# Queries, keys and values of two pairs per load, last tokens in token-major order, and expert weights issued from pair 22

## The chip, the cores and the metric

One Trainium2 chip, one NeuronCore. The time is device microseconds of one execution of the program; the kernel before takes 402.2 us, the median of three runs (401.68 to 403.0).

## The reference

Attention with a relative position bias, then a mixture of experts with hash routing. There are 8 batches, 8 heads, 576 tokens and a head dimension of 64, all inputs in float32.

```
scores = q @ k.T / 8 + bias_table[bucket(|i - j|)]     # per batch and head, 576 x 576
attn   = softmax(scores);  x = attn @ v                # x: 4608 tokens x 512
e      = token_ids * 2654435761 % 8                    # expert of each token
out    = relu(x @ w1[e]) @ w2[e]                       # w1: 512 x 1024, w2: 1024 x 512
```

## The kernel before

The work goes by pairs of heads: 8 batches of 4 pairs, 32 pairs. Of a head's 576 tokens 512 are held as 2 tiles (`NT`) of 128 partitions, each partition with two neighbouring tokens (512 bytes in float32). The last 64 tokens of each head, 32 double rows (`RU`), are packed for all four pairs of a batch into one tile, the "rest".

For each pair GpSimd casts q, k and v from float32 to float16 (`cast_qk`, L225; `cast_v`, L236), TensorE transposes q and k (`transpose_qk`, L370), and VectorE copies the results out of PSUM. Then come five steps g of scores: products of q and k, the bias added by further matmuls, and one exponential of 128x1024 on ScalarE (L506). The products with v (`av_steps`, L511) follow some one to two pairs later, nine matmuls at each step, and VectorE divides by the row sums (L546, L547) into `x_all`. The rest of a batch is cast by VectorE (`cast_rest`, L246, at step 3 of the second pair of the batch before it), transposed (`transpose_rest`, L388) and used with its batch.

The order of the work is written out by hand for all five engines (L580 to L769): what stands in the program is the order of each engine's queue. Loads, the rest, the token ids and the zero fills of the scatter table `t_xperm` stand in SyncE's queue. `pair_start(n)` (L693) puts there at the start of pair n: the rest of the next batch if n opens a batch (`load_rest`, L199, eight DMAs), q, k and v of pair n+4 (`load`, L183, six DMAs of 128 KB, one per tensor and head), the token ids at n = 4 (`route_load`, L264, six DMAs), and one fill of 514 KB for n from 2 to 11. A load waits until the buffer it overwrites (four per tensor, one pair each) has been cast. GpSimd gets at the same place the casts of q and k of pair n+3, from pair 12 on two indirect scatters of finished rows (`dispatch`, L561), and the first weights of two experts: w1 at pairs 20 and 25, w2 at pairs 22 and 28 (L713 to L720; 2 MB each in float32, cast to float16 on the way).

From pair 6 on the routing goes in small steps on VectorE, one per g. After the attention the experts run one after another on TensorE, with rows gathered by expert from `t_xperm`.

The prologue (L584 to L666) loads pairs 0 to 3, the rest of batch 0 and the bias tables in a written-out order on SyncE's and ScalarE's queues.

Of the kernel before, what the change touches and what calls it, by code (L numbers as in the profile page):

```python
# [11 lines left out]
F32 = mybir.dt.float32  # L12
# [19 lines left out]
def kernel(  # L32
# [11 lines left out]
    nc = tc.nc  # L44

    B, H, S, D = q.shape
# [6 lines left out]
    P = 128  # L53
    NPAIR = H // 2
# [95 lines left out]
    with tc.tile_pool(name="at", bufs=1) as at, tc.tile_pool(  # L150
# [29 lines left out]
        qf, kf, vf, qh, kh = {}, {}, {}, {}, {}  # L180
        qr, kr, vr = {}, {}, {}

        def load(n, which="qkv", eng=None):  # L183
            b, m = pairs[n]
            for key, dst, src in (("q", qf, q), ("k", kf, k), ("v", vf, v)):
                if key not in which:
                    continue
                dst[n] = at.tile([P, 2, NT, 2 * D], F32, name=key + "f",
                                 bufs=4)
                for hh in range(2):  # L190
                    (eng or nc.sync).dma_start(  # L191
                        out=dst[n][:, hh, :, :],
                        in_=bass.AP(
                            src.tensor, (b * H + 2 * m + hh) * S * D,
                            [[2 * D, P], [2 * P * D, NT], [1, 2 * D]],
                        ),
                    )

        def load_rest(b, which="qkv", eng=None):  # L199
            for key, dst, src in (("q", qr, q), ("k", kr, k)):  # L200
                if key not in which:
                    continue
                dst[b] = at.tile([P, 2, 2 * D], F32, name=key + "r", bufs=1)
                for hh in range(2):
                    (eng or nc.sync).dma_start(  # L205
                        out=dst[b][:, hh, :],
                        in_=bass.AP(
                            src.tensor, ((b * H + hh) * S + NB4) * D,
                            [[2 * S * D, NPAIR], [2 * D, RU], [1, 2 * D]],
                        ),  # L210
                    )
            if "v" in which:
                vr[b] = at.tile([P, NPAIR, D], F32, name="vr", bufs=1)
                for hh in range(2):
                    for c in range(2):
                        r0 = D * hh + RU * c
                        (eng or nc.sync).dma_start(  # L217
                            out=vr[b][r0 : r0 + RU, :, :],
                            in_=bass.AP(
                                v.tensor, ((b * H + hh) * S + NB4 + c) * D,  # L220
                                [[2 * D, RU], [2 * S * D, NPAIR], [1, D]],
                            ),
                        )

        def cast_qk(n, qeng=None, keng=None):  # L225
            for dst, src, name, eng in ((qh, qf, "qh", qeng),
                                        (kh, kf, "kh", keng)):
                dst[n] = at.tile([P, KT, 2, D], F16, name=name, bufs=2)
                (eng or nc.gpsimd).tensor_copy(  # L229
                    out=dst[n][:, :, :, :].transpose([0, 2, 1, 3]),  # L230
                    in_=src[n][:, :, :, :].rearrange(
                        "p h t (c d) -> p h (t c) d", c=2
                    ),
                )

        def cast_v(n):  # L236
            nc.gpsimd.tensor_copy(
                out=va[n % 3][:, :, :D],
                in_=vf[n][:, :, :, :].rearrange(
                    "p h t (c d) -> p (h t c) d", c=2  # L240
                ),
            )
# [145 lines left out]
        def transpose_rest(b):  # L388
            pr = aux(0, [P, 2, 2, P], F16, "pr")
            for i, key in enumerate("kq"):  # L390
                for c in range(2):
                    nc.tensor.transpose(
                        out=pr[:, i, c, :],
                        in_=rh[b, key][:, c, :, :].rearrange(
                            "p h d -> p (h d)"
                        ),
                        identity=ident[:, :],
                    )
            for hh in range(2):
                nc.vector.tensor_copy(  # L400
                    out=kzr[b % 2][D * hh : D * hh + D, :,
                                   D * hh : D * hh + D].rearrange(
                        "p m (c u) -> p c m u", c=2
                    ),
                    in_=pr[D * hh : D * hh + D, 0, :, :].rearrange(
                        "p c (m u) -> p c m u", m=NPAIR
                    ),
                )
            nc.vector.tensor_copy(
                out=qtr[b % 2][:, :, :].rearrange(  # L410
                    "p m (c u) -> p c m u", c=2
                ),
                in_=pr[:, 1, :, :].rearrange(
                    "p c (m u) -> p c m u", m=NPAIR
                ),
            )

# [163 lines left out]
            E_ALL.PE, E_ALL.Activation, E_ALL.Pool, E_ALL.SP, E_ALL.DVE,  # L581
        })
        guard.__enter__()
        load(0, "k")  # L584
        warm = at.tile([1, 1], F32, name="warm")
        nc.vector.memset(warm[:, :], 0.0)
        nc.scalar.activation(
# [6 lines left out]
        nc.gpsimd.memset(ebsb[:, :, :], 0.0)  # L594
        nc.scalar.dma_start(out=ohsb[:, :], in_=OH_d.ap())
        nc.scalar.dma_start(out=idents[:, :, :], in_=I128_d.ap())
        load(0, "q")
        load_rest(0, "kq", nc.scalar)

        cast_qk(0, nc.vector, nc.vector)  # L600
# [20 lines left out]
                ),  # L621
            )

        load(0, "v", nc.scalar)
        load_band(0, 2, nc.scalar)
        load(1, "qk")
        for hh in range(2):
            for c in range(2):
                r0 = D * hh + RU * c
# [25 lines left out]
        cast_v(0)  # L655
        load_band(2, 4, nc.sync)
        load_rest(0, "v")
        load(1, "v")
        cast_vrest(0)
        load(2)  # L660
        load_band(4, H, nc.sync)
        cast_qk(2)
        load(3)
        nc.sync.dma_start(out=msk[:, :], in_=MSK_d.ap())
        nc.sync.dma_start(out=cnt[:, :], in_=CNT_d.ap())
        nc.sync.dma_start(out=tok[:, :], in_=TOK_d.ap())  # L666

        FILLS = 10

# [23 lines left out]
        def pair_start(n):  # L693
            b, m = pairs[n]
            if b + 1 < B and m == 0:
                load_rest(b + 1)
            if n + 4 < NP:
                load(n + 4)
            if n == 4:
                route_load()  # L700
            if 2 <= n < 2 + FILLS:
                fill_table(n - 2)
            if n + 3 < NP:
                cast_qk(n + 3)
            if b + 1 < B and m == 2:
                cast_vrest(b + 1)
            if n >= 6 and pairs[n - 2][1] == 0:
                waiting.extend((pairs[n - 6][0], t) for t in range(NIT))
            if n >= 12:
                for _ in range(2 if n < NP - 2 else 4):  # L710
                    if waiting:
                        dispatch(*waiting.pop(0))
            if n == 20:  # L713
                load_w1(0)
            if n == 22:
                load_w2(0)
            if n == 25:
                load_w1(1)
            if n == 28:
                load_w2(1)  # L720

        def behind(n, g):
            G = NIT * n + g
# [261 lines left out]
```

## Time and profile before

| | before |
|---|---|
| median of three runs | 402.2 us |
| the profiled execution | 404.91 us, span 403.1 us |
| mean granted TensorE clock | 0.939 of full speed |
| busy: TensorE, ScalarE, GpSimd, VectorE | 338.6, 202.1, 160.9, 124.8 us |
| DMA | 72.87 MB in 94548 packets, 181 GB/s mean |

The span is what the hardware profiler saw of one execution; the execution's own time is slightly longer. PE is TensorE's matmul, PEld its weight loads, DVE VectorE, ACT ScalarE, POOL GpSimd and SP SyncE; a "q" behind the name is that engine's sequencer, which issues DMAs. L506 is line 506 of the kernel. Busy time is an average over attention and experts, which have different limits.

### The profile page before, as it was taken

Reading aid. Unit: us, or ns where it says so; the run is one execution under the profiler, and the core shown is the slowest. Engines: PE = TensorE matmul, PEld = TensorE weight load, DVE = VectorE, ACT = ScalarE, POOL = GpSimd, SP = SyncE. Lnnn points to the kernel's source line nnn. Section 1 sums busy time; section 2 is a strip of 40 time slices with the busy share of each in tenths; the row PEclk is TensorE's granted clock in tenths of the full one; section 3 lists DMA queues with packets and bytes.
Section 4 is the critical chain, followed back from the end, with each engine's and each line's share of the span. In section 5 each row is a group of like instructions: output and inputs, shape, how many; then the busy total and the mean of one; then the engine's idle time right before and its main releaser. Section 6 shows DMA issues by size and latency. Waiting matters only on the chain.

```text
span 403.1 us, 9232 instructions
## 1 busy us (share of the span) xinstructions
PE 338.6 (84%) x3796; PEld 210.3 (52%) x3796; DVE 124.8 (31%) x322; ACT 202.1 (50%) x235; POOL 160.9 (40%) x229
## 2 busy tenths in 40 slices
PE   2648994999999998688968708999999999999990
PEld 0224663566665664455545506665657565656650
DVE  2103442644343534134313301323141413223220
ACT  1262991898887879277847602231405051422310
POOL 6112413414358664591657230243343415141331
PEclk9995996899999999699989967999999999999997
DMA  5885958979694858987978143499999999996211
GB/s 155 204 226 167 251 157 197 266 192 269 179 271 140 240 176 181 261 144 185 196 209 136 51 126 116 76 205 154 262 170 248 216 184 270 152 261 117 89 69 63
DMA packets 94548, 72.87 MB, mean 181 GB/s; under 512 B 15223, under 2 KB 85655, under 8 KB 94496
## 3 DMA queue, kind: packets, MB, share of 16 engines
q1 hardware_dynamic: 74720, 40.13, 36.9%
q0 software_dynamic: 17664, 30.96, 36.8%
q10 hardware_dynamic: 2112, 1.09, 1.0%
q8 instruction: 32, 0.52, 0.6%
q14 instruction: 20, 0.16, 0.1%
HBM read 69.47 MB, written 21.03 MB: 225 GB/s over the span
## 4 chain that ended last, share of the span: by engine, by line
PE 61%; DMA 17%; SPq 10%; issue 4%; DVE 3%; POOL 2%; ACT 1%; ACTq 1%; POOLq 0%; DVEq 0%
PE hps L815 17%; PE ops L833 17%; PE px L537 7%; PE ps L441 7%; DMA kf<-in_k_dram 7%; PE ps L464 5%; SPq L191 5%; DMA kr<-in_k_dram 4%; PE pqk L376 3%; PE xps L794 2%; SPq L205 2%; SPq L217 2%; DMA xpn<-t_xperm 1%; DMA btb<-t_f 1%; DVE x_all L547 1%
## 5 line engine op out<-in xcount | busy, mean ns | idle before, releaser
L506 ACT ACTIVATE att<-ps 128x1024 f16<-128x1024 f32 x160 | 152.9, 1027 | 64.0 <-PE ps L464 41.8
L821 ACT ACTIVATE h<-hps 128x640 f16<-128x640 f32 x64 | 45.1, 704 | 112.8 <-PE hps L815 112.2
L441 PE MATMUL ps<-btb,idents 128*128 128x384 f16 (+1 forms) x384 | 80.0, 294 | 2.6 <-DMA btb<-t_f 2.3
L833 PE MATMUL ops<-w2t,h 128*128 128x512 f16 x320 | 72.7, 379 | 0.0
L815 PE MATMUL hps<-xpt,w1t 128*128 128x320 f16 x512 | 72.4, 302 | 0.1
L841 POOL DMA_INDIRECT out_dram<-ok,xpn x40 | 39.2, 980 | 57.4 <-DVE ok L840 50.6
L815 PEld LDWEIGHTS <-w1t 128*128 128x128 f16 x512 | 50.6, 99 | 21.3 <-issue 0.3
L537 PEld LDWEIGHTS <-att 128*128 128x128 f16 x1408 | 58.0, 100 | 6.9 <-issue 1.2
L537 PE MATMUL px<-va,att 128*128 128x65 f16 x1280 | 59.4, 197 | 0.5 <-DVE rcp L546 0.4
L833 PEld LDWEIGHTS <-h 128*128 128x128 f16 x320 | 30.7, 98 | 33.5
L562 POOL DMA_INDIRECT t_xperm<-x_all,ds x40 | 39.5, 987 | 20.5 <-DVE rcp L546 7.7
L464 PE MATMUL ps<-qt,kt 64*128 64x512 f16 x256 | 45.1, 401 | 2.8 <-ACT att L506 2.4
L229 POOL CAST qh<-qf 128x512 f16<-128x512 f32 x31 | 19.5, 628 | 68.0 <-DMA qf<-in_q_dram 48.3
L441 PEld LDWEIGHTS <-idents 128*128 128x128 f16 x464 | 29.4, 100 | 29.1 <-issue 27.6
L840 DVE COPY ok<-ops 128x512 f32<-128x512 f32 x40 | 27.7, 692 | 46.9 <-PE ops L833 46.9
L798 DVE COPY xpt<-xps 128x640 f16<-128x640 f16 x32 | 15.0, 489 | 74.6 <-PE xps L794 60.0
L382 DVE COPY kt<-pqk 128x512 f16<-128x512 f16 x32 | 13.6, 425 | 64.7 <-PE pqk L376 45.3
L376 PE MATMUL pqk<-idents,kh 128*128 128x128 f16 x128 | 13.7, 236 | 22.1 <-POOL kh L229 15.8
L547 DVE TENSOR_TENSOR x_all<-px,rcp 128x384 f16<-128x384 f32 x64 | 31.4, 491 | 2.2
L464 PEld LDWEIGHTS <-kt 64*128 64x128 f16 x512 | 15.0, 96 | 30.9 <-issue 27.5
L546 DVE RECIPROCAL rcp<-px 128x6 f32<-128x6 f32 x64 | 12.0, 187 | 57.1 <-PE px L537 48.5
L133 POOL DMA_DIRECT2D w1t<-in_moe_w_dram x8 | 6.5, 810 | 52.3 <-PE xps L794 52.3
(71 smaller groups left out, 244.5 us busy)
## 6 DMA issues: line engine op xcount, KB each, us to landing
kf<-in_k_dram SPq DMA_DIRECT2D x64, 128.0 KB
qf<-in_q_dram SPq DMA_DIRECT2D x64, 128.0 KB
w1t<-in_moe_w_dram POOLq DMA_DIRECT2D x8, 1024.0 KB
w2t<-in_moe_w_dram POOLq DMA_DIRECT2D x8, 1024.0 KB
vf<-in_v_dram SPq DMA_DIRECT2D x62, 128.0 KB
t_xperm<-zx SPq DMA_DIRECT2D x10, 514.0 KB
xpn<-t_xperm SPq DMA_DIRECT2D x8, 642.5 KB
vr<-in_v_dram SPq DMA_DIRECT2D x32, 32.0 KB
```

The lines of the kernel that those rows point to most:

```text
L376: nc.tensor.transpose(out=pqk[:, i, o : o + P], in_=src[n][:, t, :, :].rearrange("p h d -> p (h d)"), identity=ident[:, :],)
L441: nc.tensor.matmul(out=out, lhsT=idents[:, which, :], rhs=rhs, start=start, stop=True, skip_group_check=True,)
L464: nc.tensor.matmul(out=ps[:, hh, o : o + rhs.shape[1]], lhsT=lhsT, rhs=rhs, start=not biased and (g < KT or t == 0), stop=True, skip_group ...
L506: nc.scalar.activation(out=att[:, g, :, :], in_=ps[:, :, :], func=AF.Exp, bias=0.0, scale=scale,)
L537: nc.tensor.matmul(out=po, lhsT=lhsT, rhs=rhs, start=(i == 0), stop=(i == len(todo) - 1), skip_group_check=True,)
L547: nc.vector.tensor_tensor(out=x_all[:, b, its[0] : its[0] + ni, :DM].rearrange("p t (m h d) -> p t m h d", h=2, m=NPAIR)[:, :, m, :, :], i ...
L562: sc_in = nc.gpsimd.indirect_dma_start(out=xperm_d.ap()[:, :], out_offset=bass.IndirectOffsetOnAxis(ap=ds2[:, B * t + b : B * t + b + 1], ...
L815: nc.tensor.matmul(out=hps[:, nr, :NR], lhsT=w1h[:, kt, ts(ft, P)], rhs=xt[e][:, kt, ts(nr, NR)], start=(kt == 0), stop=(kt == NPT - 1),)
L821: nc.scalar.activation(out=h1[:, ft, :].rearrange("p (r n) -> p r n", r=NRC), in_=hps[:, :, :NR], func=AF.Relu, bias=0.0, scale=1.0,)
L833: nc.tensor.matmul(out=ops[:, :], lhsT=h1[:, ft, ts(kc, P)], rhs=w2h[:, ft, :], start=(ft == 0), stop=(ft == NFT - 1),)
L840: nc.vector.tensor_copy(out=ok[:, :], in_=ops[:, :])
L841: so = nc.gpsimd.indirect_dma_start(out=out[:, :], out_offset=bass.IndirectOffsetOnAxis(ap=xn[e][:, kc, DM:XW].bitcast(I32), axis=0), in_= ...
```

## The change

It does four things. `load` takes an index of two pairs and loads four heads of a tensor with two DMAs of 256 KB, one for each token tile T, instead of four DMAs of 128 KB, one for each head; the first two pairs are loaded as halves. There are three buffers of two pairs instead of four of one. At the start of an even pair n, SyncE gets q and k of pairs n+6 and n+7, then v of pairs n+4 and n+5. In the prologue q and k of pairs 4 and 5 stand ahead of the rest of batch 1. In `load_rest` the source pattern of q and k goes over the 32 double rows first and the four pairs second, so that the partition order is token-major, and the copies in `transpose_rest` undo that order as they read PSUM. The first weights are issued at pairs 22, 24, 26 and 28, as w1, w2, w1, w2.

```diff
-        def load(n, which="qkv", eng=None):
-            b, m = pairs[n]
+        def load(j, which="qkv", eng=None, h0=0, h1=4):
...
-                dst[n] = at.tile([P, 2, NT, 2 * D], F32, name=key + "f",
-                                 bufs=4)
-                for hh in range(2):
+                if j not in dst:
+                    dst[j] = at.tile([P, 4, NT, 2 * D], F32, name=key + "f",
+                                     bufs=3)
+                for T in range(NT):
                     (eng or nc.sync).dma_start(
-                        out=dst[n][:, hh, :, :],
+                        out=dst[j][:, h0:h1, T, :],
                         in_=bass.AP(
-                            src.tensor, (b * H + 2 * m + hh) * S * D,
-                            [[2 * D, P], [2 * P * D, NT], [1, 2 * D]],
+                            src.tensor, (4 * j + h0) * S * D + 2 * P * D * T,
+                            [[2 * D, P], [S * D, h1 - h0], [1, 2 * D]],
...
-                            [[2 * S * D, NPAIR], [2 * D, RU], [1, 2 * D]],
+                            [[2 * D, RU], [2 * S * D, NPAIR], [1, 2 * D]],
...
-                in_=vf[n][:, :, :, :].rearrange(
+                in_=vf[n // 2][:, 2 * (n % 2) : 2 * (n % 2) + 2].rearrange(
...
-                        "p c (m u) -> p c m u", m=NPAIR
+                        "p c (u m) -> p c m u", m=NPAIR
...
-        load(0, "k")
+        load(0, "k", None, 0, 2)
...
-        load(0, "v", nc.scalar)
+        load(0, "v", nc.scalar, 0, 2)
         load_band(0, 2, nc.scalar)
-        load(1, "qk")
+        load(0, "qk", None, 2)
...
         load_band(2, 4, nc.sync)
         load_rest(0, "v")
-        load(1, "v")
+        load(0, "v", None, 2)
         cast_vrest(0)
-        load(2)
+        load(1, "qk")
         load_band(4, H, nc.sync)
         cast_qk(2)
-        load(3)
+        load(1, "v")
...
+        load(2, "qk")
...
-            if n + 4 < NP:
-                load(n + 4)
+            if n % 2 == 0 and n + 6 < NP:
+                load(n // 2 + 3, "qk")
+            if n % 2 == 0 and n + 4 < NP:
+                load(n // 2 + 2, "v")
...
-            if n == 20:
-                load_w1(0)
-            if n == 22:
-                load_w2(0)
-            if n == 25:
-                load_w1(1)
-            if n == 28:
-                load_w2(1)
+            if n >= 22 and n % 2 == 0 and n < 30:
+                (load_w2 if n % 4 == 0 else load_w1)((n - 22) // 4)
```

## Rows read from the trace of the kernel before

**Rows 1.** The page, busy tenths of 40 slices: TensorE and the DMA engines.
```profile
PE   2648994999999998688968708999999999999990
...
DMA  5885958979694858987978143499999999996211
```

**Rows 2.** The page, chain that ended last, shares of the span by line.
```profile
PE hps L815 17%; PE ops L833 17%; PE px L537 7%; PE ps L441 7%; DMA kf<-in_k_dram 7%; PE ps L464 5%; SPq L191 5%; DMA kr<-in_k_dram 4%; PE pqk L376 3%; PE xps L794 2%; SPq L205 2%; SPq L217 2%; DMA xpn<-t_xperm 1%; DMA btb<-t_f 1%; DVE x_all L547 1%
```

**Rows 3.** ScalarE's timeline: start, us, instruction, count, idle before and its releaser.
```profile
24.40 3.77 ACT L506 ACTIVATE att<-ps 128x1024 f16<-128x1024 f32 x4 [0.27 <-PE ps L464]
34.34 1.02 ACT L506 ACTIVATE att<-ps 128x1024 f16<-128x1024 f32 x1 [6.17 <-PE ps L464]
35.51 1.02 ACT L506 ACTIVATE att<-ps 128x1024 f16<-128x1024 f32 x1
39.40 1.94 ACT L506 ACTIVATE att<-ps 128x1024 f16<-128x1024 f32 x2 [2.87 <-PE ps L464]
...
70.53 1.02 ACT L506 ACTIVATE att<-ps 128x1024 f16<-128x1024 f32 x1 [7.80 <-PE ps L464]
...
78.47 3.77 ACT L506 ACTIVATE att<-ps 128x1024 f16<-128x1024 f32 x4 [0.41 <-PE ps L464]
...
100.24 3.77 ACT L506 ACTIVATE att<-ps 128x1024 f16<-128x1024 f32 x4 [0.40 <-PE ps L464]
104.33 4.83 ACT L506 ACTIVATE att<-ps 128x1024 f16<-128x1024 f32 x5 [0.32 <-PE ps L464]
...
168.09 1.02 ACT L506 ACTIVATE att<-ps 128x1024 f16<-128x1024 f32 x1 [7.22 <-PE ps L464]
...
181.82 7.52 ACT L506 ACTIVATE att<-ps 128x1024 f16<-128x1024 f32 x8 [0.56 <-PE ps L441]
...
210.13 5.87 ACT L506 ACTIVATE att<-ps 128x1024 f16<-128x1024 f32 x6 [5.16 <-PE ps L464]
...
220.39 7.44 ACT L506 ACTIVATE att<-ps 128x1024 f16<-128x1024 f32 x8 [0.35 <-PE ps L441]
```

**Rows 4.** SyncE's timeline, the DMAs it issues: start, us, target and source, count.
```profile
11.59 1.76 SPq L630 DMA_DIRECT2D btr<-t_f  x4
...
47.99 0.47 SPq L672 DMA_DIRECT2D t_xperm<-zx  x1
...
59.46 3.55 SPq L274 DMA_DIRECT2D te<-in_moe_token_ids_dram  x6
```

**Rows 5.** Windows: busy us (count) of each engine, granted clock, DMA share, GB/s.
```profile
core 0: us, PE busy (x) PEld busy (x) DVE busy (x) ACT busy (x) POOL busy (x), PEclk, DMA share, GB/s
244.80:394.40 149.60, 148.71 (x979) 90.12 (x977) 41.77 (x70) 45.05 (x64) 48.67 (x51) 0.99 0.78 168
...
29.50:32.50 3.00, 1.58 (x22) 1.58 (x23) 0.50 (x2) 0.00 (x0) 1.18 (x2) 0.50 0.21 58
...
37.00:40.00 3.00, 3.00 (x27) 1.46 (x26) 1.47 (x5) 0.60 (x1) 1.78 (x3) 0.57 0.86 248
...
64.00:65.00 1.00, 0.00 (x0) 0.00 (x0) 0.21 (x2) 0.00 (x0) 0.00 (x0) 0.50 1.04 395
...
61.00:63.50 2.50, 0.40 (x2) 0.01 (x1) 0.00 (x0) 1.73 (x2) 1.00 (x2) 0.99 0.85 6
...
154.00:164.00 10.00, 5.51 (x82) 3.17 (x79) 3.32 (x12) 6.58 (x7) 2.49 (x4) 0.92 1.05 209
...
10.00:20.00 10.00, 5.96 (x36) 2.81 (x36) 1.92 (x6) 2.81 (x3) 1.26 (x3) 1.00 0.87 203
```

**Rows 6.** The chain in order of time: start, us, what the end waited for.
```profile
31.02 4.28 DMA kr<-in_k_dram
...
155.10 9.04 DMA kf<-in_k_dram
```

**Rows 7.** VectorE's groups by line and form: busy us, mean ns, idle before.
```profile
L382 DVE COPY kt<-pqk 128x512 f16<-128x512 f16 x32 | 13.6, 425 | 64.7 <-PE pqk L376 45.3 <-issue 11.9 <-PE prr L441 3.9
...
L409 DVE COPY qtr<-pr 128x256 f16<-128x256 f16 x8 | 2.3, 292 | 0.1
```

**Rows 8.** The issues of w1 on GpSimd: ns min/median/max, first and last start.
```profile
L133 POOL DMA_DIRECT2D w1t<-in_moe_w_dram x8: 803/803/848, 154.4 to 348.3; - x8
```

More of the change, by code (lines that the diff above doesn't have):

```diff
@@ L230, in cast_qk @@
                     out=dst[n][:, :, :, :].transpose([0, 2, 1, 3]),
-                    in_=src[n][:, :, :, :].rearrange(
+                    in_=src[n // 2][:, 2 * (n % 2) : 2 * (n % 2) + 2].rearrange(
                         "p h t (c d) -> p h (t c) d", c=2
@@ L413, in transpose_rest @@
                 in_=pr[:, 1, :, :].rearrange(
-                    "p c (m u) -> p c m u", m=NPAIR
+                    "p c (u m) -> p c m u", m=NPAIR
                 ),
@@ L596 @@
         nc.scalar.dma_start(out=idents[:, :, :], in_=I128_d.ap())
-        load(0, "q")
+        load(0, "q", None, 0, 2)
         load_rest(0, "kq", nc.scalar)
```

## Prediction

> **What bounds the kernel now.** I read the busy shares first, then the chain of waits, then ScalarE's timeline over the attention, then SyncE's queue, and last the DMA share of short stretches. TensorE and the DMA engines are both busy most of the time, so shares settle nothing [rows 1]. The chain splits the run in two [rows 2]. From 244.8 to 394.4 the experts run with TensorE busy for 148.7 of 149.6 us [rows 5]: nothing in the diff touches that, and I leave it as it is. All that can change is the attention before it, with its 160 exponentials of 128x1024, five for each of 32 pairs.
>
> Those exponentials are the clock of the attention. In an undisturbed stretch 24 of them take from 78.47 to 104.33, which is 1.077 us each or 5.4 us a pair. But the 48 from 39.40 to 100.24 (exponential 13, in pair 2, to exponential 60, the last of pair 11) take 60.8 us, and the 100 from 100.24 to 227.83 take 127.6 [rows 3]. The difference sits in a few holes: 11.2 us from the end at 28.17 to 39.40 with two exponentials (2.1 us) in it, then 7.80, 7.22 and 5.16 us [rows 3]. What ends late there? Twice in the chain it is a load of q, k or their last tokens: 4.28 us for kr at 31.02, and 9.04 us for kf at 155.10 [rows 6]. The hole of 7.80 us follows the token ids (te), which SyncE begins to issue only at 59.46 and needs 3.55 us for [rows 4].
>
> Two reasons show why the loads are late. First, SyncE issues without a pause: from 11.59 to 48.46 it puts out 61 DMAs, 0.60 us each [rows 4], so a pair's six loads cost it some 3 us of the 5.4. Second, while qr and kr land, the DMA share is 0.21 and 58 GB/s move, where loads of q, k and v run at a share of 0.86 and 248 GB/s, that is 288 GB/s at a full share [rows 5]. A share of 0.21 is about 3.4 of 16 engines. The Trainium skill, in "DMA: Bandwidth & Descriptors", section "Why a DMA increments its semaphore by 16 and not by 1", says that a DMA runs on the largest number of engines up to 16 that divides the slowest dimension of both sides: 4 for the old order of last tokens, 16 for the new; the share of 0.21 agrees with the first, and no run here yet shows the second.
>
> **Last tokens in token-major order.** The source pattern goes from 4 pairs x 32 rows to 32 rows x 4 pairs, with the same 512 B runs. The price afterwards is bounded by 4.28 us (as kr lands now) and 0.9 us (256 KB of qr and kr at 288 GB/s). I take 0.9, because the loads of q, k and v, whose slowest dimension is also long, are the nearest row. SyncE's issues (eight a batch) stay.
>
> The copies behind the transposes now read PSUM with a step of four. A copy of 512 columns takes 425 ns and one of 256 takes 292 [rows 7], 133 ns for 256 elements. The Trainium skill, in "VectorE: DVE Perf Modes", section "Mode 2×_1P", says that two results per cycle need a step of one; by it each of the three copies would take some 133 ns longer, an estimate, and the sum would be 3.2 us higher if none were hidden. From the rows alone the cost lies between 0 and one more slope of 133 ns: 24 copies, 0 to 3.2 us. The results are wanted a pair and more later, so only VectorE's next reciprocal can feel it; I take 0.7 us.
>
> **Loads of two pairs.** About 90 of 192 issues of q, k and v fall away, some 54 us of SyncE's time at 0.60 each, which lie beside other work and count only through lateness. Three buffers of two pairs let SyncE be about five pairs ahead of the casts of q and k: the loads for pairs n+6 and n+7 wait for the cast of pair n+1, which GpSimd has in its queue at pair n-2, and those of v (pairs n+4 and n+5) for the cast of pair n-1, in its queue at pair n-2 too. Behind these waits stand last tokens, te and fills, so SyncE can't run further ahead than that, which still leaves each of them over three pairs. The price is order: in the one queue 1.05 MB (q and k of pairs 4 and 5) now stand ahead of the last tokens of batch 1, and later q, k and v stand ahead of te.
>
> Start: q and k of pairs 2 and 3 come together, so those of pair 2 land up to 512 KB later, 1.8 us at 288 GB/s, and the transposes at the start of pair 1 wait; but pair 3's no longer do. The last tokens of batch 1 come behind 3.7 us more of data and land 3.4 us faster once they start (4.28 less 0.9), and SyncE reaches them some 2 us earlier. VectorE stands at their cast either way. Sum: exponential 13 starts 1.9 us earlier (bounds: 4 earlier, 1.5 later).
>
> Pairs 2 to 11: 48 exponentials at 1.077 are 51.7 us instead of 60.8, a gain of 9.1. Does the queue hold that pace? From the last tokens of batch 1 (about 34 us) to those of batch 4 it carries 10.35 MB of loads, 36 us at 288, ten fills of 514 KB, 13.5 us at the 380 GB/s of a full share [rows 5], and te at some 2 us (61 to 63.5 at a share of 0.85 [rows 5]): they land near 87 and are wanted in pair 13, near 97. Those of batches 2 and 3 have 3 us in hand. Only te has none: behind 5.2 MB of loads (18 us), two fills (2.7 us) and its own 2 us it lands near 57 at the earliest, and VectorE, which does nothing else until it has it, wants it at pair 6, near 58. I charge 1.5 us.
>
> Pairs 12 to 31: 127.6 us now. GpSimd's scatters stand in this stretch, and its own pace is slower: 50 exponentials from 104.33 to the hole that begins at 160.87, 1.13 us each. Against that pace 6.9 us are the hole ended at 168.09 (7.22 less the usual 0.3); the 10 from there to 181.82 take 13.7, 2.4 too many; the 20 to 210.13 take 28.3, 5.7 too many; the 8 to 220.39 take 10.3, 1.2 too many [rows 3]. Together 16.2.
>
> **Weights from pair 22.** Four issues move on GpSimd's queue: from pairs 20, 22, 25, 28 to 22, 24, 26, 28. Each costs about 0.8 us of GpSimd [rows 8] as before. While one is in flight the share is 1.05 [rows 5], and q and k issued beside it were what came 9 us late. With five pairs in hand (27 us) they aren't missed. By the new pace pair 22 starts near 146 and pair 28 near 180, so the last is in long before the experts begin near 221. I charge 1 us for what they still hinder.
>
> **Sum**: 1.9 + 9.1 - 1.5 + 16.2 - 1.0 - 0.7 = 24.0 us. The profiled execution took 404.9 us (span 403.1), 2.7 above the median of the runs, 402.2; I take the difference from the median: **378 us**.
>
> **Rivals.**
> A. Late te and last tokens. If the queue runs at the 233 GB/s of the start (203 at a share of 0.87 [rows 5]), te lands 4 us later and batch 1's last tokens 0.8: 383. For it: both stand behind deeper prefetch, in a queue with 53 us of work between 34 and 91. Against: full shares show 288.
> B. The weights still win. If q, k or last tokens stay late beside weights, the holes of 7.22 and 5.16 us remain: 378 + 12 = 390. For: the DMA share is 1.05 there; against: the earlier issue.
> C. No deeper prefetch in effect, SyncE held by its waits for the casts, or the holes only moving on to GpSimd: 402. Against it speaks that the casts of the reused buffers come four pairs before.
> D. Slower: a DMA across four heads moves less per microsecond than one over a head's two neighbouring blocks. At 175 GB/s the 10.35 MB take 59 us instead of 36 and the gain is gone; below that it is slower, at 160 by about 5 us: 407. Against: the runs stay 512 B, and the share says that engines, not addresses, are short; no row shows this pattern.
>
> **How the numbers follow.** Forecast 0.68; down to 369 without the three charges (3.2), with the start at its good bound (2.1) and the last 100 exponentials at 1.077 too (3.7); up to 388 with the start (3.4), the copies (2.5) and te (4) at their bad ones. A 0.10, B 0.11, C 0.05, D 0.06. The range is 369 to 391, which takes in A and B and leaves out C, D and the edges. About 0.3% (1.2 us) is what a measurement can tell: faster 0.90 (forecast, A, B and a little of C), same 0.04, slower 0.06.
>
> **What would show it.** Right: half the q, k and v issues; a DMA share far over 0.21 while qr and kr land; no hole over 3 us between exponential 13 and the last; SyncE pausing on GpSimd's casts instead of issuing without end. Step by step: exponential 61 near 91 us, the last ending near 204, the experts from 221. Wrong: holes ended by te or the cast of last tokens (A), by kf beside weights (B), or loads that take clearly more than 288 GB/s allows (D).

## The result, and the profile after

The changed kernel takes 397.62 us (397.42 to 398.83) against 402.2: ratio 0.9892, interval 0.9852 to 0.9933. It is faster, by 4.6 us instead of the 24.0 forecast, and lies outside the range of 369 to 391. The profiled execution took 397.42 us (span 395.6); that of before stood 2.7 us above its median, so the two traces differ by 7.5 us. The marks of the forecast split them:

| stretch | before | after | gain | forecast |
|---|---|---|---|---|
| start to exponential 13 | 39.40 | 36.77 | 2.6 | 1.9 |
| exponentials 13 to 60 | 60.8 | 63.6 | -2.8 | 9.1 - 1.5 = 7.6 |
| the 100 from exponential 61 | 127.6 | 120.1 | 7.5 | 16.2 - 1.0 - 0.7 = 14.5 |
| from the last one to the end | 175.3 | 175.1 | 0.2 | 0 |

The page of the changed kernel, busy tenths, chain by line, and issues (target, queue, count, KB), answers to [rows 1, 2]:

```profile
PE   2667994999988889799998429999999999999990
...
DMA  5998978999879487399871160799999999994221
...
PE hps L812 18%; PE ops L830 17%; PE ps L441 11%; PE px L537 11%; PE ps L464 9%; PE pqk L376 4%; PE xps L791 3%; DVE x_all L547 2%; DMA qr<-in_q_dram 2%; SPq L191 2%; PE ps L498 2%; ACT att L506 2%; SPq L274 2%; DMA btb<-t_f 1%; DMA vf<-in_v_dram 1%
...
qf<-in_q_dram SPq DMA_DIRECT2D x30, 256.0 KB
kf<-in_k_dram SPq DMA_DIRECT2D x30, 256.0 KB
vf<-in_v_dram SPq DMA_DIRECT2D x30, 256.0 KB
```

Of the 192 issues of q, k and v 102 are left, these 90 and 12 halves for the first two pairs. The loads of k and kr, 7% and 4% of the chain before, are no longer among its entries; the chain stands on TensorE's attention lines, and line 274, the issue of the token ids, has risen to 2%. ScalarE's timeline after, against [rows 3]:

```profile
36.77 1.02 ACT L506 ACTIVATE att<-ps 128x1024 f16<-128x1024 f32 x1 [2.69 <-PE ps L464]
...
70.02 1.02 ACT L506 ACTIVATE att<-ps 128x1024 f16<-128x1024 f32 x1 [8.06 <-PE ps L464]
...
100.39 1.94 ACT L506 ACTIVATE att<-ps 128x1024 f16<-128x1024 f32 x2 [0.41 <-PE ps L464]
...
140.28 1.94 ACT L506 ACTIVATE att<-ps 128x1024 f16<-128x1024 f32 x2 [1.99 <-PE ps L441]
...
165.50 1.94 ACT L506 ACTIVATE att<-ps 128x1024 f16<-128x1024 f32 x2 [2.01 <-PE ps L441]
...
211.22 9.27 ACT L506 ACTIVATE att<-ps 128x1024 f16<-128x1024 f32 x10 [3.50 <-PE px L537]
```

The holes of 7.22 and 5.16 us are closed, but that of 7.80 us stands, now 8.06, and small holes of 1 to 2 us come in every batch: the 50 exponentials of pairs 12 to 21 take 61.2 us (100.39 to 161.6), 1.22 each, where before they took 1.13. SyncE's timeline ([rows 4]) and VectorE's show what ends the hole of 8.06:

```profile
28.13 1.51 SPq L205 DMA_DIRECT2D qr<-in_q_dram  x2
29.75 1.19 SPq L205 DMA_DIRECT2D kr<-in_k_dram  x2
...
55.28 6.73 SPq L274 DMA_DIRECT2D te<-in_moe_token_ids_dram  x6
```

```profile
59.64 0.42 DVE L409 COPY qtr<-pr 128x256 f16<-128x256 f16 x1
63.85 0.18 DVE L286 TENSOR_SCALAR te<-te 128x40 int32<-128x40 int32 x1 [3.78 <-DMA te<-in_moe_token_ids_dram]
```

VectorE stands until 63.85. Before, it stood until 64.76:

```profile
64.76 0.18 DVE L286 TENSOR_SCALAR te<-te 128x40 int32<-128x40 int32 x1 [4.32 <-DMA te<-in_moe_token_ids_dram]
```

Windows after ([rows 5]; columns as there):

```profile
29.50:32.50 3.00, 3.00 (x52) 1.94 (x48) 0.76 (x2) 2.29 (x3) 0.62 (x1) 1.00 0.74 200
...
237.90:388.00 150.10, 148.09 (x972) 89.45 (x969) 41.28 (x69) 45.07 (x64) 49.68 (x52) 0.99 0.78 169
```

The share while the last tokens land is 0.74 instead of 0.21. That isn't theirs alone: q and k of pairs 4 and 5, issued just ahead of them, land in the same stretch. The experts are as they were. VectorE's groups by form, against [rows 7]:

```profile
L400 DVE COPY kzr<-pr 64x256 f16<-64x256 f16 x16 | 6.8, 422 | 4.4 <-PE pr L392 4.3
...
L249 DVE CAST qrh<-qr 128x256 f16<-128x256 f32 x8 | 5.1, 637 | 1.8 <-DMA qr<-in_q_dram 1.8
L249 DVE CAST krh<-kr 128x256 f16<-128x256 f32 x8 | 3.7, 460 | 0.7 <-DMA kr<-in_k_dram 0.6
L409 DVE COPY qtr<-pr 128x256 f16<-128x256 f16 x8 | 3.4, 425 | 0.1
```

The copy of qtr went from 292 to 425 ns, the 133 ns of the bound and of the rule cited there. The cast of qrh, which the change doesn't touch, went from 304 to 637 ns; this is its line before:

```profile
L249 DVE CAST qrh<-qr 128x256 f16<-128x256 f32 x8 | 2.4, 304 | 1.6 <-DMA qr<-in_q_dram 1.6
```

Last, all engines around a pair of scatters, start and us:

```profile
137.44 0.98 POOL L562 DMA_INDIRECT t_xperm<-x_all,ds  x1 [0.28 <-POOL vt L259]
...
138.36 0.22 PE L537 MATMUL px<-vt,rr 128*128 128x130 f16 x1
...
138.72 0.97 POOL L562 DMA_INDIRECT t_xperm<-x_all,ds  x1 [0.30 <-issue]
...
138.84 0.60 PE L464 MATMUL ps<-qt,kt 64*128 64x512 f16 x4
138.89 0.42 DVE L409 COPY qtr<-pr 128x256 f16<-128x256 f16 x1
...
140.22 0.18 DVE L546 RECIPROCAL rcp<-px 128x4 f32<-128x4 f32 x1 [0.91 <-PE ps L441]
140.28 1.02 ACT L506 ACTIVATE att<-ps 128x1024 f16<-128x1024 f32 x1 [1.99 <-PE ps L441]
```

The last product of px ends at 138.58 and the scores at 139.44, and VectorE is free from 139.31; yet VectorE and ScalarE go on only at 140.22 and 140.28, half a microsecond behind the end of the second scatter (139.69).

### The profile page after: what moved, and what is told of

Read it like the earlier page. It is cut to its first block, busy times and chain, and to the rows that moved or that the text cites. A ratio compares the mean times of both kernels' runs of the same rounds, so it can differ in the third digit from the quotient of the medians.

```text
span 395.6 us, 9129 instructions
## 1 busy us (share of the span) xinstructions
PE 337.3 (85%) x3796; PEld 207.1 (52%) x3796; DVE 133.2 (34%) x322; ACT 202.5 (51%) x235; POOL 160.7 (41%) x229
## 4 chain that ended last, share of the span: by engine, by line
PE 75%; DMA 8%; DVE 5%; SPq 4%; issue 2%; ACT 2%; POOL 1%; POOLq 0%; ACTq 0%; DVEq 0%
PE hps L812 18%; PE ops L830 17%; PE ps L441 11%; PE px L537 11%; PE ps L464 9%; PE pqk L376 4%; PE xps L791 3%; DVE x_all L547 2%; DMA qr<-in_q_dram 2%; SPq L191 2%; PE ps L498 2%; ACT att L506 2%; SPq L274 2%; DMA btb<-t_f 1%; DMA vf<-in_v_dram 1%
## 5 line engine op out<-in xcount | busy, mean ns | idle before, releaser
L537 PEld LDWEIGHTS <-att 128*128 128x128 f16 x1408 | 56.6, 99 | 7.2 <-issue 1.4
L537 PE MATMUL px<-va,att 128*128 128x65 f16 x1280 | 58.1, 195 | 0.9 <-issue 0.4
L237 POOL CAST va<-vf 128x512 f16<-128x512 f32 x32 | 19.8, 619 | 40.3 <-PE px L537 30.3
L464 PEld LDWEIGHTS <-kt 64*128 64x128 f16 x512 | 14.0, 95 | 30.9 <-issue 27.8
```

What stands on the lines that cost most here:

```text
L237: nc.gpsimd.tensor_copy(out=va[n % 3][:, :, :D], in_=vf[n // 2][:, 2 * (n % 2) : 2 * (n % 2) + 2].rearrange("p h t (c d) -> p (h t c) d", ...
L464: nc.tensor.matmul(out=ps[:, hh, o : o + rhs.shape[1]], lhsT=lhsT, rhs=rhs, start=not biased and (g < KT or t == 0), stop=True, skip_group ...
L537: nc.tensor.matmul(out=po, lhsT=lhsT, rhs=rhs, start=(i == 0), stop=(i == len(todo) - 1), skip_group_check=True,)
```

## The experiments

Theories at the start: the token ids' own hole (against the loads of q and k as its cause), and in the late stretch the scatters against GpSimd's casts, which now wait for transposes. "Late" is the time of the 100 exponentials from exponential 61 to the end of the last (120.1 after, 127.6 before), E61 the start of the 61st; both from ScalarE's timeline of each trace. The kernel before, run beside each group, had medians of 402.98 (e1 to e4), 396.0 (e5 to e8), 401.8 (e9 to e12), 400.81 (e13 to e16) and 402.34 us (e17, e18); each group ran on a chip of its own. Where no ratio is given, the kernel ran once.

| run | us | ratio to before | E61 | late |
|---|---|---|---|---|
| e1 | 392.09 | 0.9778 [0.967, 0.9887] | 93.3 | 122.4 |
| e2 | 384.53 | | 101.2 | 108.4 |
| e3 | 383.11 | | 99.7 | 108.5 |
| e4 | 393.44 | 0.979 [0.9703, 0.9877] | 99.2 | 119.5 |
| e5 | 382.52 | | 99.9 | 107.2 |
| e6 | 383.67 | 0.9702 [0.964, 0.9763] | 98.5 | 108.7 |
| e7 | 378.24 | 0.9584 [0.9526, 0.9642] | 92.8 | 107.6 |
| e8 | 379.47 | 0.9583 [0.9541, 0.9626] | 94.3 | 108.0 |
| e9 | 397.59 | 0.9908 [0.9867, 0.9949] | 99.5 | 122.0 |
| e10 | 400.62 | | 100.1 | 123.2 |
| e11 | 401.53 | 1.0003 [0.9957, 1.0048] | 99.7 | 123.4 |
| e12 | 393.23 | 0.9801 [0.9702, 0.9899] | 92.4 | 123.4 |
| e13 | 381.72 | 0.9574 [0.9512, 0.9636] | 99.0 | 108.4 |
| e14 | 397.53 | 0.995 [0.9914, 0.9986] | 102.0 | 120.0 |
| e15 | 399.31 | 0.9966 [0.9924, 1.0008] | 98.9 | 124.0 |
| e16 | 402.06 | 1.0046 [1.0003, 1.0088] | 99.4 | 125.8 |
| e17 | 376.0 | 0.9372 [0.9315, 0.943] | 92.3 | 108.4 |
| e18 | 392.05 | 0.977 [0.9702, 0.9837] | 100.2 | 117.6 |

**e1**, the changed kernel with the token ids earlier:

```diff
-            if n == 4:
+            if n == 0:
                 route_load()
```

> The changed kernel with the six loads of the token ids issued at the start of pair 0 instead of pair 4, behind the last tokens of batch 1 and the loads that stand there. Theory (the hole of 8 us before exponential 35 is nothing but the late token ids): the ids land near 42 us instead of 63.7, no hole over 1.5 us is left before exponential 35, exponential 61 starts near 93 instead of 100.4, and the time falls by 6 to 8 us, to about 390. Rival (the queue is simply full up to there, and something else behind the fills is late next, the last tokens of batch 2 or q and k of pairs 8 to 11): exponential 61 moves by less than 3 us and the time by less than 2.

E61 comes 7.1 us sooner. ScalarE's timeline of e1 has 2.45 us where 8.06 stood:

```profile
64.66 5.75 ACT L506 ACTIVATE att<-ps 128x1024 f16<-128x1024 f32 x6 [2.45 <-PE ps L464]
```

The late token ids made all of the hole of the changed kernel but these 2.45 us. It cost more than its length: behind it, from 64 to 70 us, the granted clock of the changed kernel is 0.50, the lower of the two levels (1.2 GHz), after four microseconds in which TensorE was busy for 0.63; in e1 it is 1.00 (2.4 GHz) from 60 to 72. Pair 7, which follows, takes 7.0 us in the changed kernel and 5.5 in e1.

**e2, e3**, the changed kernel and the kernel before without the scatters of pairs 12 to 31:

```diff
-                        dispatch(*waiting.pop(0))
+                        waiting.pop(0)
```

> The changed kernel without the 35 scatters of finished rows that GpSimd issues from pair 12 on (only the five of the last batch stay), so the experts work on rows of zeros; only the attention is read, from exponential 61 to the last. Theory S (while GpSimd issues an indirect scatter, what TensorE signals reaches VectorE and ScalarE late): the 100 exponentials take about 108 to 110 us instead of 120, 5.4 us a pair, and no reciprocal starts over 0.1 us after its last product unless VectorE itself was busy. Rival D (slower copies and casts on VectorE at each batch) and rival Q (GpSimd's casts wait for the transposes): over 116 us, gaps of 2 us remain.

> The kernel before without the same 35 scatters; the experts again work on zeros and only the attention is read. Theory S, with the phase of the scatters set by what GpSimd waits for: the stretch of 50 exponentials that took 1.13 us each before the hole at 160.9 comes to 1.08, 2.5 us less in 50, while the holes of 7.2 and 5.2 us behind the weights stay; the 100 exponentials take 120 to 125 us instead of 127.6. If scatters cost the same whatever their phase, the gain here equals that of the changed kernel without scatters, 10 to 12 us.

Both fall to the same late time, and e3, of which I had expected 120 to 125, has a single hole over 1.5 us there (3.51). Without its rows being written the kernel before needs no faster loads on this chip.

**e4**, a third buffer for GpSimd's casts of q and k:

```diff
-                dst[n] = at.tile([P, KT, 2, D], F16, name=name, bufs=2)
+                dst[n] = at.tile([P, KT, 2, D], F16, name=name, bufs=3)
```

> The changed kernel with three buffers instead of two for the float16 q and k that GpSimd casts, so that a cast needn't wait for the transposes of the pair two before. Theory Q (that wait, 33 us in total, holds up the scatters and casts of v behind it in GpSimd's queue, and so the attention): the 100 exponentials from number 61 take 112 to 115 us instead of 120, the time falls by 5 to 8 us. Theory S (the scatters cost by where they fall, and an earlier cast only moves them): the stretch changes by less than 4 us, in either direction.

The late time is that of the changed kernel (119.5 against 120.1): the casts' wait is not what slows the pace. That the whole came out about 4 us below the changed kernel's 397.6 is not explained; E61 is only 1.2 us sooner, and the changed kernel itself was not run on this chip.

**e5, e6**, the old pattern of the last tokens and the old copies back in the changed kernel (e5 without the scatters as e2 too):

```diff
-                            [[2 * D, RU], [2 * S * D, NPAIR], [1, 2 * D]],
+                            [[2 * S * D, NPAIR], [2 * D, RU], [1, 2 * D]],
...
-                        "p c (u m) -> p c m u", m=NPAIR
+                        "p c (m u) -> p c m u", m=NPAIR
```

> The changed kernel without the 35 scatters of the attention (experts on zeros, only the attention is read) and with the old order of last tokens, the copies unit-step again. Theory D (with the scatters gone, the pair before each batch takes 6.4 us instead of the 5.4 of the kernel before, because of three copies 133 ns longer and two casts on VectorE that now run beside GpSimd's and take 0.5 us more together): the copies are back at 289 ns, the casts stay slow, and that pair takes 6.0 us, the 100 exponentials 107 instead of 108.4. Rival (last tokens on a quarter of the engines come late and hold VectorE): pairs over 7 us, DVE waiting on DMA kr or qr.

> The changed kernel with only the old order of last tokens (scatters in place). If the new order is worth what the prediction took (last tokens of batch 1 some 3 us earlier, the queue 4 us freer at each of seven batches), this is slower than the changed kernel by 3 us or more, with a DMA share near 0.25 where qr and kr land alone. If the engines were only idle where nothing needed them, it is within 2 us of the changed kernel after the start, and the 100 exponentials from number 61 take 118 to 121.

The third pair of a batch, in which the last tokens of the next are transposed and copied, takes 6.1 us in e5 against 6.4 in e2: the slower copies cost 0.3 us a batch. At the start the old pattern costs 3 to 5 us (pair 3 at 45.8 in e6, at 41.1 in e7). But e6 has its scatters, and a late time of 108.7: here they cost 1.5 us (107.2 without them in e5), and my expectation of 118 to 121 missed. On this chip the change is worth 12.3 us even without the new order of last tokens (396.0 to 383.67).

**e7, e12** (the same kernel on two chips) and **e8**, all with early token ids; e7 and e12 with the scatters behind the cast of v at step 2, e8 with the scatters where they were and the rest of batch 1 ahead of q and k of pairs 4 and 5:

```diff
+            if g == 2 and n >= 12:
+                for _ in range(2 if n < NP - 2 else 4):
+                    if waiting:
+                        dispatch(*waiting.pop(0))
```

```diff
-        load(2, "qk")
...
+            if n == 0:
+                load(2, "qk")
```

> The token ids at pair 0 and, besides, the two scatters of a pair issued behind GpSimd's cast of v at step 2 instead of at the pair's start. Theory S (a scatter costs by where it falls among TensorE's signals): the 100 exponentials move by 4 us or more from the 122 of the run with the ids alone; as ScalarE has no bias matmuls of the next pair to wait for in mid-pair, downwards, to 112 to 118, and the time to 383 to 388. Rival (each scatter costs the same wherever it stands): 120 to 124, the time within 2 us of the run with the ids alone.

> The token ids at pair 0 and, besides, the last tokens of batch 1 issued ahead of q and k of pairs 4 and 5. Theory (the 1.05 MB put ahead of them are what holds pair 2, 10 us long in the run with the ids alone): qr lands 3 to 4 us earlier, pair 3 starts near 38 to 39 instead of 41.8, exponential 61 near 90, and the time falls by 2 to 4 us against the run with the ids alone. Rival (q and k of pairs 2 and 3, which come as one, or the bias table set the start): pair 3 moves by less than 1 us.

e8 leaves the scatters in place and is as quick as e7 there, so their place is not it; at the start it gains nothing (pair 3 at 42.4, expected 38 to 39), though exponential 13 starts at 33.9: a hole of 5.64 us follows it. All engines in e8 around the same two scatters:

```profile
127.54 0.98 POOL L562 DMA_INDIRECT t_xperm<-x_all,ds  x1 [0.17 <-DVE krh L249]
...
128.83 0.97 POOL L562 DMA_INDIRECT t_xperm<-x_all,ds  x1 [0.30 <-issue]
...
129.05 0.22 PE L537 MATMUL px<-vt,rr 128*128 128x130 f16 x1
...
129.53 0.61 PE L464 MATMUL ps<-qt,kt 64*128 64x512 f16 x4
...
129.92 0.17 DVE L546 RECIPROCAL rcp<-px 128x4 f32<-128x4 f32 x1
129.96 1.94 ACT L506 ACTIVATE att<-ps 128x1024 f16<-128x1024 f32 x2 [0.91 <-PE ps L464]
```

From the start of the last px product to the exponential it is 0.91 us here and 1.92 in the changed kernel above (from the start of the four score products 0.43 and 1.44), with scatters of the same length and spacing. The granted clock doesn't tell the two chips apart: it is 1.00 over the late stretch of the changed kernel and of e7. So I asked whether kernel or chip decides.

**e9, e10, e12**, the changed kernel, the kernel before and e7's kernel together on another chip:

> The changed kernel, nothing edited, to read its late attention on another chip: are the scatters dear in the kernel or on the chip? Theory S (the scatters cost by where they stand in the program: at the pair's start, with nothing ahead of them): the 100 exponentials from pair 12 take 119 to 122 us again, as in its first trace, reciprocals start up to 1.5 us behind the products with v, and the time is 397. Rival H (the scatters are dear on one chip and nearly free on another): here the 100 exponentials take 108 to 111 us, some 5.3 to 5.6 a pair, with reciprocals at once behind the products; the time is then 386 to 389. Under both the hole in front of pair 7 (14 us for pair 6), which the token ids make, stays.

> The kernel before, nothing edited, for its trace on the same chip as the changed one. Theory S: 127 us for the 100 exponentials from pair 12 as in its first trace, with three holes in front of pairs 23, 27 and 30, and a time near 403. Rival H: 112 to 120 us for them, the holes behind the weights small (pairs 22, 26 and 29 near 6 to 8 us), as in the run of it without scatters, and a time of 388 to 396; what the change gains on this chip in this stretch is then under 8 us.

> The changed kernel with the token ids issued at pair 0 and the two scatters of a pair behind the cast of v at its third step: the fastest so far (378.24 us on a chip where the kernel before took 396.0), again, on the chip of the unchanged kernels. Theory S: the 100 exponentials from pair 12 take 107 to 109 us wherever the unchanged kernel takes 119 to 122, and the time is 378. Rival H: it takes as long as the unchanged kernel in this stretch within 2 us, so on a dear chip 118 to 121 us and a time near 391, on a cheap one 108 and 378; what it gains over the unchanged kernel is the 6 to 7 us of the token ids.

Rival H holds: the kernel that took 378.24 us, late 107.6, takes 393.23 here, late 123.4. From the last exponential to the end both need the same 175 us. e9 repeats the result (0.9908). But split by the marks of the first table, its gain over e10 is 1.2, -0.6, 1.1 and 1.0 us: 4.4 of the 7.5 of the late stretch there is that the kernel before took longer in that trace (127.6 against 123.2). e12 is 4.4 us faster than e9: E61 comes 7.0 us sooner, and the late stretch is 1.4 longer.

**e11**, e1's edit made on the kernel before:

> The kernel before with the six DMAs of the token ids issued at the start of pair 0 instead of pair 4 and nothing else. If the token ids alone made the hole of 7.8 us in front of pair 7, as the same edit of the changed kernel shows, pair 6 takes 7 to 8 us instead of 13.2, exponential 61 starts near 94 instead of 100.24, and the time falls by 5 to 6 us: the same gain as the whole change, without it. Rival: before the change q and k of pairs 7 and 8 are late beside the fills too, so the hole shrinks by under 2 us.

No gain: the rival held. ScalarE's and GpSimd's timelines of e11 show what ends late next:

```profile
68.46 1.94 ACT L506 ACTIVATE att<-ps 128x1024 f16<-128x1024 f32 x2 [2.50 <-PE ps L464]
```

```profile
61.96 0.61 POOL L229 CAST qh<-qf 128x512 f16<-128x512 f32 x1 [5.23 <-DMA qf<-in_q_dram]
...
66.81 0.61 POOL L229 CAST qh<-qf 128x512 f16<-128x512 f32 x1 [2.81 <-DMA qf<-in_q_dram]
```

Late q stood behind the late token ids. The change removes the one wait, e1's edit the other, and only both together bring 7 us (E61 on this chip: 100.1 with neither, 99.7 and 99.5 with one, 92.4 with both).

**e13**, the scatters of the changed kernel as plain DMAs:

```diff
-            sc_in = nc.gpsimd.indirect_dma_start(
-                out=xperm_d.ap()[:, :],
...
+            r0, nr = P * (NIT * b + t), len(tok_of[t])
+            sc_in = nc.gpsimd.dma_start(
+                out=xperm_d.ap()[r0 : r0 + nr, :], in_=x_all[:nr, b, t, :]
+            )
```

> The changed kernel with each indirect scatter into the scatter table replaced by a plain DMA of the same rows from the same place in GpSimd's queue, into rows fixed beforehand (so the experts get other tokens than the routing says; the bytes, the queue, the waits and the order are the same, the row addresses are not read from a tensor). Theory I (the indirect instruction holds the engines up while it is on GpSimd, on a chip where scatters are dear): the 100 exponentials from pair 12 take 108 to 110 us as without any scatter, and the time is 384 to 387 against the 397.6 of the changed kernel. Rival T (the traffic of the rows does it): 118 to 122 us and 396 to 398. Should the chip be one where scatters are cheap (kernel before near 396), both theories give 108 to 110 us and it tells nothing.

Late 108.4, on a chip where e14, the changed kernel but for the weights' places, takes 120.0: theory I. GpSimd's groups by form from 100 to 220 us, of the changed kernel and then of e13 (columns as in [rows 7]):

```profile
L562 POOL DMA_INDIRECT t_xperm<-x_all,ds x35 | 34.6, 989 | 8.5 <-issue 5.4 <-POOL vt L259 1.2 <-DMA qf<-in_q_dram 0.3
```

```profile
L563 POOL DMA_DIRECT2D t_xperm<-x_all x38 | 20.5, 545 | 9.5 <-DVE rcp L546 9.5
```

The bytes aren't what holds the engines up. A plain write is also shorter on GpSimd and its rows lie together, so which trait of the indirect one does it stays open.

**e14, e15**, the old places of the weights in the changed kernel, the new ones in the kernel before:

```diff
-            if n >= 22 and n % 2 == 0 and n < 30:
-                (load_w2 if n % 4 == 0 else load_w1)((n - 22) // 4)
+            if n == 20:
+                load_w1(0)
...
```

> The changed kernel with the first weights at pairs 20, 22, 25 and 28 again, and all else as changed. Theory L (the deeper loads, not the weights' places, closed the holes in front of pairs 23, 27 and 30): holes over 3 us don't come back, the time is that of the changed kernel within 1.5 us (396 to 399 on a dear chip). Rival W (the places closed them): two holes of 4 to 7 us are back behind pairs 20 and 25, and the time is 402 to 408. My forecast counted their place as a cost of 1 us, nothing more.

> The kernel before with the first weights at pairs 22, 24, 26 and 28 and nothing else. Theory L: the holes only move with the weights, by one or two pairs, and the time is the same within 2 us. Rival W: the holes shrink by 4 us or more together and the time falls by 3 us or more, most of the 4.6 us of the whole change.

Theory L: the holes don't come back in e14, and e15 can't be told from no change. The places of the weights bring nothing by themselves.

**e16**, the token-major last tokens alone on the kernel before (e6's edit the other way round):

> The kernel before with the last tokens of q and k in token-major order (and the copies that undo it) and nothing else. From my sum: kr lands 3.4 us sooner at the start, exponential 13 starts 2 to 3 us sooner than in the kernel before, and the 24 copies cost up to 3.2 us of VectorE, mostly hidden. Theory E (what the start gains is lost again in the hole of the token ids in front of pair 7): exponential 61 starts where it did within 1 us, and the time is the same within 1.5 us. Rival: the gain lasts, exponential 61 starts 2 us or more sooner and the time falls by 2 to 3 us.

Exponential 13 starts at 35.10, 4.3 us sooner (pair 3 2.3 us sooner, at 40.45 instead of 42.74), and E61 within 0.8 us of where it did: theory E. This run has the new order without other new loads: the cast of krh starts at 32.23 instead of 35.42, 1.7 us behind the last issue of kr instead of 3.9 (I had taken 0.9), with a DMA share of 0.35 from 29.3 to 32.2. So the order does bring the last tokens sooner, but the second half of the rule cited in the prediction, 16 engines, can't be read from such a share. What the start wins is lost in front of the token ids, and the whole is no faster (if anything 0.5% slower).

**e17, e18**, early token ids and plain writes, in the changed kernel and in the kernel before (edits of e1 and e13):

> The changed kernel with the token ids issued at pair 0 and plain writes in fixed rows in place of the indirect scatters (the experts get other tokens than the routing says). If the two terms are the whole miss, exponential 61 starts at 92 to 94, the 100 exponentials from there take 107 to 109 us, the time is 374 to 376, and the distance to my 378 is explained. Rival: taking both out at once brings up a third wait, and it stays at 378 to 382.

> The kernel before with the same two edits (token ids at pair 0, plain writes in fixed rows; the experts get other tokens than the routing says). Theory N (the deeper loads are worth something only once the token ids are out of the way): holes in front of pairs 7 and 8 behind late q, k and v as in the kernel before with early token ids alone, exponential 61 near 99.5, the 100 exponentials 108 to 110, the time 381 to 383, so that the change is worth 6 to 8 us with both out. Rival: the loads of the kernel before keep up once both are out, and it takes 375 to 378, so that the change brings under 2 us even then.

e17 takes 376.0, E61 at 92.3, late 108.4: the two waits are what holds the changed kernel up. That it comes so near to my 378 is partly luck: the 48 exponentials of the middle take 55.4 us where the forecast had 53.2, the late stretch is 4.7 us below the forecast's 113.1, and the experts, which get other rows here, are 1.9 us shorter. e18 keeps a late time of 117.6 where I had expected 108 to 110, so with both out the change is worth 16 us. GpSimd's and ScalarE's timelines of e18, where the first weights are issued:

```profile
146.73 0.78 POOL L133 DMA_DIRECT2D w1t<-in_moe_w_dram  x1
...
158.76 0.61 POOL L229 CAST qh<-qf 128x512 f16<-128x512 f32 x1 [10.64 <-DMA qf<-in_q_dram]
```

```profile
163.45 1.02 ACT L506 ACTIVATE att<-ps 128x1024 f16<-128x1024 f32 x1 [6.29 <-PE ps L464]
...
201.63 1.02 ACT L506 ACTIVATE att<-ps 128x1024 f16<-128x1024 f32 x1 [4.40 <-PE ps L464]
```

ScalarE's timeline of e17 from 158 us on has no such hole:

```profile
158.87 3.77 ACT L506 ACTIVATE att<-ps 128x1024 f16<-128x1024 f32 x4 [0.40 <-PE ps L464]
162.95 5.75 ACT L506 ACTIVATE att<-ps 128x1024 f16<-128x1024 f32 x6 [0.32 <-PE ps L464]
169.16 1.94 ACT L506 ACTIVATE att<-ps 128x1024 f16<-128x1024 f32 x2 [0.46 <-PE ps L464]
```

GpSimd stood 10.6 us for q behind w1, as k was waited for in [rows 6], and the deeper loads end that. Why e3, with no rows written at all, hardly shows these holes (the writes, or its chip) stays open.

## Why the prediction was wrong

**Start, 1.9 us: the number came out, in part by luck.** 2.6 measured at the mark, but 1.2 between e9 and e10, and only 1.4 at the start of pair 3 (42.74 and 41.31). The token-major order alone brings 4.3 at the mark and 2.3 at pair 3 (e16), so the deeper loads take back 0.9 to 1.7, where I had 1.8.

**The charge of 1.5 us for the token ids: mis-sized, 7 to 8** (7.1 from e1 to the changed kernel, 7.9 from e1 to e2 on one chip, 7.0 from e12 to e9 on another). I took them to land near 57 at the earliest, from the bytes ahead of them at 288 GB/s, and left out their issue; SyncE issued them only from 55.28 to 62.0, for 6.73 us instead of the 3.55 of [rows 4], and VectorE had them at 63.85. Why the issue became longer is not shown. I also took the hole of 7.80 us as the loads' hole with the token ids as a remainder. Both were late, one behind the other (e1, e11), and the change moved one of them. Rival A had this mechanism, but priced at 4 us of queue speed.

**Pairs 2 to 11, 9.1 us: too large by 3.6 to 4.1.** With early token ids the 48 exponentials take 55.3 to 55.8 us (e1, e12, e17, e7), a gain of 5.0 to 5.5 against 60.8. Two pairs keep them from 51.7: pair 6 takes 8.0 to 8.4 us and pair 10, the third of its batch, 6.4, instead of 5.4.

**Pairs 12 to 31, 16.2 us: the step that failed is the pace.** I wrote that the scatters stand in this stretch and took 1.13 us an exponential, read beside them in the kernel before, as what stays. It became 1.22: the 50 exponentials of pairs 12 to 21, where neither kernel has a hole over 2 us, take 61.2 us instead of 56.6. Of these 4.6 us 1.9 come without any scatter (54.7 in e2, 52.8 in e3), because the third pair of a batch takes 6.4 instead of 5.4; the copies are 0.3 of that, and the rest is not taken apart (VectorE's slower casts stand there). The other 2.7 are scatters that cost more than before (1.5 on the chip of e9 and e10, where the 50 take 61.8 and 58.4).

The holes closed as forecast, but were worth less: without the indirect scatters late is 117.6 before and 108.4 after (e18, e17), 9.2 us, and with no rows written there is no difference (e3, e2). Against plain writes the indirect scatters cost the changed kernel 11.7 us and more (120.1 and 122.0 against 108.4) and the kernel before 5.6 to 10.0 (123.2 and 127.6 against 117.6), over chips that aren't all the same. Why they cost the changed kernel more stays open. That before some of them fell into the holes that the loads made anyway is not tested, and can't be all of it, as pairs 12 to 21 had no such hole. On the one chip where they are cheap, changed kernels come to 107.6 to 108.7, under the 111.4 that the forecast left (127.6 less 16.2).

**Weights, 1.0 us: near enough.** Their places do nothing (e14, e15). **Copies, 0.7 us: too small.** The 133 ns came as worked out, 3.2 us for 24 copies; 0.3 us a batch reaches the end, 1.2 in the late stretch (108.4 in e2, 107.2 in e5). That VectorE's casts of last tokens would become slower I didn't ask, and so put at nothing.

Rival B is refuted (one hole of 3.50 us is left, with px as its releaser, no load), and e17 runs without any load in front of a hole of the late stretch. C is refuted too: GpSimd's casts of q and k waited 65.8 us for their loads before and 12.9 after, no pause of SyncE for a cast of GpSimd's is longer than 3.0 us, and the wait that moved on to GpSimd (33.0 us for transposes) is not what slows the pace (e4). So is D: from 35 to 42 us, while loads across four heads run, 296 GB/s move. Set against the forecast, 24.0 less 10.4 in the middle and 7.0 in the late stretch, plus 0.7 at the start and 0.2 at the end, is the 7.5 between the traces; that is the first table read again, and the test of the terms is e17.

A version that beats both kernels is e7's (and e12's): 378.24 us against 396.0, and 393.23 against 401.8 and the 397.59 of the changed kernel.

## What to carry over

Ask of every hole how many waits stand one behind the other in it: a small load in the same queue (the token ids, 6.7 us of issue) can hide everything that larger loads win. A pace read beside waits isn't the pace that is left without them; measure the other work of a stretch alone before it is put into the sum. Compare a start at more than one mark, as a gain at one exponential can be lost at the next. And where the same kernel differs by 15 us between chips, an experiment needs the unchanged kernels on its own chip.

## What the runs showed of the hardware

- While indirect scatters are on GpSimd, VectorE and ScalarE can take up finished products of TensorE late, on some chips and hardly on others: 1.92 against 0.91 us from the last product to the exponential, 123.4 against 107.6 us for the same 100 exponentials of the same kernel (e12, e7). The scatter itself takes 0.98 us on GpSimd on both. With plain writes in their place the delay is gone (0.91 us in e13; late 108.4 against 120.0 in e14 on the same chip). Which trait of the scatter does it, and what differs between the chips, no run here shows.
- VectorE's casts of last tokens became slower without an edit, qrh from 304 to 637 ns: they now run beside GpSimd's casts, as VectorE's and GpSimd's timelines of the changed kernel show. The Trainium skill, in "SBUF — State Buffer", section "SBUF: two separate sides", says that the two engines share a pair of ports as an exclusive lock: where VectorE's instruction runs in a two-port mode or has two SBUF inputs, the later one waits for the whole of the other. The rows agree roughly: qrh takes 0.28 us beside no cast in the kernel before (57.87) and ends here 0.14 us behind kh, where a full wait would make it end 0.28 behind. In which mode the cast runs no run here shows.

```profile
135.69 0.74 DVE L249 CAST qrh<-qr 128x256 f16<-128x256 f32 x1
```

```profile
135.67 0.62 POOL L229 CAST kh<-kf 128x512 f16<-128x512 f32 x1
```
